# Key scores spread to step 84 of a batch, with the first piece's query scores all behind them

## The chip, the cores and the metric

The kernel runs on one core of one Trainium2 chip. The metric is the device time of one execution in microseconds, the median of several runs.

## The reference

For each of four batches the reference computes an attention through 49 agents, and then a feed-forward layer with a cosine gate over all 49,920 rows. Cut to what matters:

```python
def sm(a, b):
    s = scale * (a @ b.transpose(0, 2, 1))
    s = s - s.max(-1, keepdims=True)
    e = np.exp(s)
    return e / (e.sum(-1, keepdims=True) + 1e-09)
a2k = sm(agents, k)            # 49 x 12480 in each batch
agent_v = a2k @ v
q2a = sm(q, agents)            # 12480 x 49 in each batch
x = (q2a @ agent_v)            # all batches: 49920 x 128
h = x @ w_in                   # 49920 x 2048
return (h * np.cos(h)) @ w_out
```

## The kernel before

The 12,480 rows of a batch are cut into 13 groups of 960. The feed-forward layer runs as one long loop of 832 steps: a group takes 16 steps (two halves of 480 rows, eight pairs of 128-wide slices of the 2048 columns), and a batch takes 208. In this text a step is counted from the start of its batch, and eight steps that begin at a multiple of eight are called an octet, by the number of their first step.

In each step TensorE makes two products `ph` (the 2048-wide layer, with `w_in` already folded into the agents' values), ScalarE takes the cosine `c` of them, VectorE makes `r = (c - 1) * ph`, and four steps later TensorE multiplies `r` by `w_out` into `po`. Once in eight steps two further products (`po<-pT,b`) add what was subtracted. `ph` has three buffers in PSUM, so TensorE can be at most three steps ahead of VectorE.

Between the steps stands the attention, written out by hand into a table of steps:

- Key scores of the next batch: 13 jobs, one for each group. A job has two halves (`part_scores`, L232), each of four matmuls into the one PSUM tile `one` (`ps_1`, a single buffer, L610). After the second half ScalarE copies the scores to `s`, and VectorE updates the running maximum `run`.
- Query scores: the same two halves. ScalarE copies them to `e`, VectorE finds each row's maximum `mx` (`query_ranked`, L686) and GpSimd subtracts it. In the four steps of a burst VectorE does both straight from PSUM (`query_kept`, L673).
- The maxima's chain: `top` reduces `run` to `m` on VectorE, `across` transposes it on TensorE into `one`, VectorE makes `mx` and `mxw` of it, `spread` multiplies it back into `one`, and VectorE copies it to `mxb`. Then GpSimd subtracts `mxb` from all 13 groups of `s` (`shift`, L392).
- At step 112 (24 or 26 in a first part, 8 in later batches) comes a burst: ScalarE leaves the cosine for the exponentials of a whole piece of queries and, at step 112, of all key groups, with a table load before and after.

`plan` puts a call at a fixed step. `job` puts it in a queue with a first step and a due step; `spread_over` hands out such steps evenly. A queue entry may begin only in steps whose place in the octet is 0, 1, 2, 4 or 6 (`free`, L1114), one half at a time, the one with the earliest due step first. Inside each engine the order of instructions is the order in which the table is run. `early[b]` is the piece of queries whose burst is at step 112 of batch b; two of its six groups are made in the burst before, and the other four are the first piece's query scores of which the change speaks. The fourth batch has no next batch, and the changed lines leave it as it was.

Of the kernel before, what the change touches and what calls it, by code (L numbers as in the profile page):

```python
# [37 lines left out]
S0 = 24  # L38
T1 = 112
T2 = 8  # L40
K1 = 76
V1 = 196
NV = 5
WL = 19
# [1 line left out]
SH = 1  # L46
# [26 lines left out]
QP = 1  # L73
QD = 1
EA = 0
QS = 0
QV = 1
PJ = 1
QI = 5
# [43 lines left out]
N0 = 2  # L123
N1 = 4
N2 = 2
# [19 lines left out]
def agent_attention_cos_ffn(ctx, tc, qT, kT, v, agT, w_in, w_out, outT):  # L145
    nc = tc.nc
    NB, _, N = qT.shape
# [8 lines left out]
    NG = N // GRP  # L156
# [31 lines left out]
    pe, dve, act, pool = (Ordered(x) for x in (nc.tensor, nc.vector, nc.scalar, nc.gpsimd))  # L188
# [122 lines left out]
    class Agents:  # L311
# [42 lines left out]
            self.rank(g)  # L354

        def rank(self, g):
            if g == 0:
                dve.tensor_copy(self.run, self.part(g))
            else:
                dve.tensor_max(self.run, self.run, self.part(g))  # L360
# [5 lines left out]
            return self.s[:, g * GT:(g + n) * GT, :]  # L366

        def top(self):
            self.m = self.sb.tile([TT, NA], F32, name="m", bufs=1)
            dve.tensor_reduce(self.m, self.run.rearrange("p t a -> p a t"), axis=AX.X, op=ALU.max)  # L370

# [166 lines left out]
    class First(Fast):  # L538
# [30 lines left out]
                dve.tensor_reduce(self.m[:, 0], self.run.rearrange("p t a -> p a t"), axis=AX.X, op=ALU.max)  # L569

        def top(self):
            dve.tensor_max(self.m[:, 0], self.m[:, 0], self.m[:, 1])

        def across(self, pt):
# [32 lines left out]
    with ExitStack() as pools:  # L607
# [388 lines left out]
        plan, post = Plan(), Plan()  # L996
# [3 lines left out]
        def job(n, *parts, by=10 ** 6):  # L1000

            queue.append((n, len(queue), by, parts))

        def spread_over(lo, hi, by, jobs):

            for i, parts in enumerate(jobs):
                job(lo + (hi - lo) * i / len(jobs), *parts, by=lo + (by - lo) * (i + 1) / len(jobs) + 1)

        def q_lot(n):
            return [(query, n, k, piece_of[n]) for k in range(2)]  # L1010
# [8 lines left out]
        def burst(n, piece, two=(), ab=None, also=()):  # L1019

            shut.update(range(n, n + SHUT))
            wide_at.update(range(n, n + SHUT + WX))
            for i in range(0, len(two), 2):
                post(n + i // 2 * BD, query_two, two[i:i + 2], piece_of[two[0]])
            if ab is not None:
                for g, k in lots:
                    post(n, pinned_exp, ab, g, k)
            post(n, query_exp, piece)
            if also:
                post(n, query_exp, also)  # L1030
                post(n + 12, query_sums, also, 0, len(also))
                post(n + 20, query_inverse, also, 0, len(also))
            s0 = SF if ab is not None else SD1
            for k in piece[:s0]:
                post(n, query_sum, k)
            post(n, query_inverse, piece, 0, s0)
            m = n + SM
            if ab is not None:
                for k in piece[s0:]:
                    post(m, query_sum, k)  # L1040
                    m += 1
                post(m, query_inverse, piece, s0, len(piece))
                return
            for i in range(s0, len(piece), ST):
                j = min(i + ST, len(piece))
                post(m, query_sums, piece, i, j)
                m += 1
            post(m + (SR if n < T3 + (NB - 1) * PER else SZ), query_inverse, piece, s0, len(piece))
# [12 lines left out]

        plan(K1 + 10, fill_ones)
        for n, k in enumerate(LC):
# [4 lines left out]
        early = [pieces[2 * b + 2] for b in range(NB)]  # L1068
# [3 lines left out]
        for b in range(NB):  # L1072
            o = b * PER
            go, stop = o + (T1 if b < NB - 1 else T3), o + PER + T2
            last = OG and b == NB - 2
            if BM and b:
                for c in range(DFF // 512):
                    if b < NB - 1 or not BZ >> c & 1:
                        post(o + BM + 3 * c, big_late)
            if OG and b == NB - 1:  # L1080
                break
            k0 = o + (T2 + K0 if b else KB)
            spread_over(k0 + (QS if b < NB - 1 else 0), go - 5, go - 1, [q_lot(n) for n in early[b][N2 if b else N0:]])
            if b == NB - 1:
                burst(go, early[b])
                for c in range(DFF // 512):
                    if BZ >> c & 1:
                        post(go, big_late)
                for i in range(FB):
                    post(go + FO, keep_warm)  # L1090
                break
            nxt = ab[b + 1]
            spread_over(k0, o + K1, o + K1 + 1, [[(nxt.scores, g, k) for k in range(2)] for g in range(NG)])
            plan(o + K1 + 2, nxt.top)
            job(o + K1 + 4, (nxt.across,), by=o + K1 + 5)
            job(o + K1 + 6, (nxt.spread,), by=o + K1 + 8)
            for g in range(NG):
                plan(o + K1 + 9 + SH * g, nxt.shift, g, 1, pool)
            burst(go, early[b], late[b][:N1], nxt)
            for g in range(0, NG, VP):  # L1100
                at = go + V0 + (o + V1 - go - V0) * g / NG
                job(at, *((nxt.values, x, k) for x in range(g, min(g + VP, NG)) for k in range(2)), by=at + 6 * VP)
            spread_over(go + QV, o + V1 + 8 if last else stop - 3, o + V1 + 8 if last else stop - 1, [q_lot(n) for n in late[b][N1:]])
            if last:
                spread_over(o + V1 + 6, stop - 1, stop - 1, [q_lot(n) for n in early[b + 1][:-2]])
                burst(stop, late[b], early[b + 1][-2:], also=early[b + 1])
            else:
                burst(stop, late[b], early[b + 1][:N2])
            i = (b + 1) % 2
            job(o + V1 + 3, (nxt.inverse,), by=o + V1 + 8)  # L1110
            job(o + V1 + 6, *((nxt.project, c, a[i]) for c in range(DFF // 512)), by=o + PER - 6)
            job(o + V1 + 7, (nxt.project_out, wio, b1[i], b2[i]), by=o + PER + 2)
# [8 lines left out]
        while queue or begun:  # L1121
# [7 lines left out]
            n, i, by, parts = x  # L1129
# [232 lines left out]
```

## Time and profile before

| | |
|---|---|
| median of 3 runs | 1167.57 us (1167.34 to 1168.55) |
| span of the profiled execution | 1171.5 us |
| TensorE matmul busy | 1127.9 us (96%) |
| VectorE busy | 1064.8 us (91%) |
| ScalarE busy | 979.0 us (84%) |
| GpSimd busy | 564.2 us (48%) |
| chain that ended last | TensorE 62%, VectorE 18%, ScalarE 12% |

The span runs from the first to the last instruction of one profiled execution; it is the only time that the page gives of that execution, and it is 3.9 us above the median of the unprofiled runs. Busy shares are averages over the whole program; the loop's stretches differ, so the rows below are taken by octets.

### The profile page before, as it was taken

The numbers are of one execution on the slowest core, as the hardware profiler recorded it, in microseconds if no ns is written. First come the engines' busy times: TensorE is split into PE (matmuls) and PEld (weight loads), VectorE is DVE, ScalarE is ACT, GpSimd is POOL, SyncE is SP. The second block draws the span as 40 slices with busy tenths as digits, with TensorE's granted clock in tenths as the row PEclk, the third lists the DMA queues.
The fourth block names the chain that finished last, engine by engine and source line by source line (L and its number), as shares of the span: only waits on it lengthen the run. The fifth ranks groups of instructions, "written<-read, shape, count | busy, mean of one in ns | idle before, by whom it ended". The sixth has DMA issues, their size and how long they took to land.

```text
span 1171.5 us, 17248 instructions
## 1 busy us (share of the span) xinstructions
PE 1127.9 (96%) x6075; PEld 925.7 (79%) x6075; DVE 1064.8 (91%) x1202; ACT 979.0 (84%) x1267; POOL 564.2 (48%) x725
## 2 busy tenths in 40 slices
PE   8989999999999999999999999999999999999996
PEld 8869888778887888777887788877888767767774
DVE  5689888989998999989999899998999899999997
ACT  3467877889889878898888888798988999999996
POOL 2012321758963311539894331175896455545551
PEclk9899999999999999999999999999999999999999
DMA  8733433143331333124241233214331100000001
GB/s 328 304 123 119 135 102 115 55 138 105 90 113 51 103 108 120 52 87 121 78 133 53 85 102 114 89 51 138 101 94 55 49 18 34 34 18 34 17 34 37
DMA packets 31631, 109.44 MB, mean 93 GB/s; under 512 B 3504, under 2 KB 4016, under 8 KB 31536
## 3 DMA queue, kind: packets, MB, share of 16 engines
q1 hardware_dynamic: 31392, 108.13, 28.5%
q8 instruction: 50, 0.82, 0.3%
q14 instruction: 45, 0.37, 0.1%
q10 hardware_dynamic: 144, 0.12, 0.0%
HBM read 82.68 MB, written 25.56 MB: 92 GB/s over the span
## 4 chain that ended last, share of the span: by engine, by line
PE 62%; DVE 18%; ACT 12%; issue 5%; DMA 1%; POOL 1%; SPq 0%; ACTq 0%; DVEq 0%
PE ph L182 26%; PE po L182 24%; DVE r L182 13%; PE one L182 13%; ACT c L182 7%; DVE rz L182 2%; ACT osb L182 1%; ACT s L182 1%; ACT e L182 1%; ACT p L182 1%; ACT L182 1%; DVE sums L182 1%; DMA c<-kT 1%; DVE e L182 1%; DMA vh<-v 1%
## 5 line engine op out<-in xcount | busy, mean ns | idle before, releaser
L182 DVE SCALAR_TENSOR_TENSOR r<-c,ph 128x960 fp32r<-128x960 f32 (+1 forms) x833 | 906.4, 1134 | 43.3 <-ACT c L182 36.5
L182 ACT ACTIVATE c<-ph 128x960 f32<-128x960 f32 x832 | 784.8, 977 | 136.6 <-PE ph L182 120.7
L182 PE MATMUL ph<-pT,a 113*128 113x480 f32 x1664 | 519.2, 393 | 16.9 <-DVE r L182 13.1
L182 PE MATMUL po<-r,w 128*128 128x480 f32 x1664 | 523.3, 396 | 5.1 <-ACT osb L182 4.9
L182 PEld LDWEIGHTS ph<-pT,a 113*128 113x128 f32 x1664 | 295.2, 189 | 129.5 <-DVE r L182 65.3
L182 PEld LDWEIGHTS po<-r,w 128*128 128x128 f32 x1664 | 292.1, 189 | 51.4 <-ACT osb L182 13.6
L182 POOL CAST pT<-p 49x480 fp32r<-49x480 f32 x102 | 59.4, 582 | 259.7 <-ACT p L182 256.9
L182 PEld LDWEIGHTS one<-ag,xt 128*120 128x120 f32 x1088 | 133.9, 184 | 12.3 <-DVE sums L182 1.5
L182 PE MATMUL one<-ag,xt 128*120 128x98 f32 x1088 | 134.4, 265 | 0.7 <-DVE b L182 0.5
L182 POOL TENSOR_TENSOR pT<-p,pT 49x480 fp32r<-49x480 f32 x102 | 124.2, 1218 | 8.2
L182 POOL TENSOR_TENSOR vh<-vt,vh 120x512 fp32r<-120x512 f32 x78 | 93.4, 1198 | 30.5 <-ACT vh L182 30.5
L182 POOL TENSOR_TENSOR p<-e,rz 120x392 f32<-120x392 f32 x51 | 43.7, 856 | 55.2 <-DVE rz L182 50.8
L182 POOL TENSOR_TENSOR e<-e,mx 120x392 f32<-120x392 f32 x25 | 21.2, 847 | 86.5 <-DVE mx L182 86.5
L182 PE MATMUL po<-pT,b 113*128 113x480 f32 x208 | 62.5, 382 | 0.0
L182 POOL TENSOR_TENSOR raw<-c,raw 128x480 f32<-128x480 f32 x23 | 28.3, 1231 | 69.9 <-ACT raw L182 69.8
L182 ACT COPY osb<-po 128x480 f32<-128x480 f32 x104 | 58.0, 557 | 2.2 <-PE po L182 2.2
L182 PEld LDWEIGHTS ph<-ag,xt 128*120 128x120 f32 x480 | 51.9, 185 | 7.2 <-DVE r L182 4.4
L182 PE MATMUL ph<-ag,xt 128*120 128x98 f32 x480 | 54.2, 269 | 2.7 <-DVE r L182 2.0
L182 PEld LDWEIGHTS one<-vh,eh 120*113 120x113 f32 x312 | 45.9, 177 | 8.3 <-POOL vh L182 2.5
L182 PE MATMUL one<-vh,eh 120*113 120x258 f32 x312 | 50.8, 284 | 1.4 <-DVE e L182 1.4
L182 POOL TENSOR_TENSOR eh<-s,eh 120x196 fp32r<-120x196 f32 x78 | 47.7, 612 | 6.3
L182 POOL CAST eh<-s 120x196 fp32r<-120x196 f32 x78 | 27.8, 356 | 32.7 <-ACT s L182 32.3
(137 smaller groups left out, 746.4 us busy)
## 6 DMA issues: line engine op xcount, KB each, us to landing
xt<-qT SPq DMA_DIRECT2D x52, 480.0 KB, 3.5
outT<-osb SPq DMA_DIRECT2D x51, 480.0 KB, 2.6
xt<-kT SPq DMA_DIRECT2D x46, 480.0 KB, 3.6
vt<-v SPq DMA_DIRECT2D x43, 512.0 KB, 3.9
c<-kT SPq DMA_DIRECT2D x6, 480.0 KB, 7.0
vh<-v SPq DMA_DIRECT2D x5, 512.0 KB, 8.0
raw<-w_in SPq DMA_DIRECT2D x2, 512.0 KB, 7.1
a<-w_in SPq DMA_DIRECT2D x2, 512.0 KB, 6.7
```

What stands on the lines that cost most here:

```text
L182: ins = f(*args, **kw)
```

## The change

The spread of the key scores ends at step 84 instead of 76. The four query groups of the first piece, which were spread over the same steps as the key scores, now begin at step 84. The chain of the maxima starts eight steps later with it and has one step more between `top` and `across` and two more between `across` and `spread`'s first step; the shifts begin at step 95 instead of 85. Nothing is computed in another way. The assertions only check that all groups have been ranked when `top` is built.

```diff
-K1 = 76
+K1 = 84
...
-QS = 0
+Q0 = 84
...
         def rank(self, g):
+            self.ranks = g + 1
...
         def top(self):
+            assert self.ranks == NG
...
             k0 = o + (T2 + K0 if b else KB)
-            spread_over(k0 + (QS if b < NB - 1 else 0), go - 5, go - 1, [q_lot(n) for n in early[b][N2 if b else N0:]])
+            spread_over(o + Q0 if b < NB - 1 else k0, go - 5, go - 1, [q_lot(n) for n in early[b][N2 if b else N0:]])
...
             spread_over(k0, o + K1, o + K1 + 1, [[(nxt.scores, g, k) for k in range(2)] for g in range(NG)])
-            plan(o + K1 + 2, nxt.top)
-            job(o + K1 + 4, (nxt.across,), by=o + K1 + 5)
-            job(o + K1 + 6, (nxt.spread,), by=o + K1 + 8)
+            k1 = o + K1
+            plan(k1 + 2, nxt.top)
+            job(k1 + 5, (nxt.across,), by=k1 + 6)
+            job(k1 + 8, (nxt.spread,), by=k1 + 10)
             for g in range(NG):
-                plan(o + K1 + 9 + SH * g, nxt.shift, g, 1, pool)
+                plan(k1 + 11 + SH * g, nxt.shift, g, 1, pool)
```

TensorE, batch 1 (the second), where the chain stands. Before, from step 79 on; `ph` and `po` are the loop's products, `one<-ident,m` is `across`, `one<-ident,mxw` is `spread`:

```order
L182 MATMUL ph<-pT_96,a_701 128x480 x2
L182 MATMUL po<-r,w_70 128x480 x2
L182 MATMUL ph<-pT_94,a_701 128x480 x2
L182 MATMUL one<-ident,m 49x120
L182 MATMUL po<-r,w_70 128x480 x2
L182 MATMUL ph<-pT_94,a_701 128x480 x2
L182 MATMUL po<-r,w_70 128x480 x2
L182 MATMUL ph<-pT_94,a_701 128x480 x2
L182 MATMUL one<-ident,mxw 120x49
```

and in the changed kernel, from step 88 to 92; `one<-ag,xt` is half a score job:

```order
L182 MATMUL one<-ag,xt 120x98 x4
L182 MATMUL po<-r,w_70 128x480 x2
L182 MATMUL ph<-pT_94,a_701 128x480 x2
L182 MATMUL one<-ident,m 49x120
L182 MATMUL po<-r,w_70 128x480 x2
L182 MATMUL ph<-pT_94,a_701 128x480 x2
L182 MATMUL one<-ag,xt 120x98 x4
L182 MATMUL po<-r,w_70 128x480 x2
L182 MATMUL ph<-pT_94,a_701 128x480 x2
```

Before, nothing but the loop stood around `across` and `spread`; now a half of a query's scores stands before `across` and the next job's half one step behind it, `one` being the same buffer, and `spread` follows three further steps on.

TensorE, batch 1, the last sixteen steps before the burst at step 112. Before, from step 96 to 100, only the loop and one transposition `one<-ident,p` of a query group's weights:

```order
L182 MATMUL ph<-pT_95,a_701 128x480 x2
L182 MATMUL po<-r,w_70 128x480 x2
L182 MATMUL ph<-pT_95,a_701 128x480 x2
L182 MATMUL po<-pT_94,b_91 128x480
L182 MATMUL po<-pT_94,b_93 128x480
L182 MATMUL po<-r,w_70 128x480 x2
L182 MATMUL ph<-pT_95,a_701 128x480 x2
L182 MATMUL one<-ident,p_100 113x120 x4
```

and in the changed kernel:

```order
L182 MATMUL ph<-pT_95,a_701 128x480 x2
L182 MATMUL one<-ag,xt 120x98 x4
L182 MATMUL po<-r,w_70 128x480 x2
L182 MATMUL ph<-pT_95,a_701 128x480 x2
L182 MATMUL one<-ag,xt 120x98 x4
L182 MATMUL po<-r,w_70 128x480 x2
L182 MATMUL ph<-pT_95,a_701 128x480 x2
L182 MATMUL po<-r,w_70 128x480 x2
L182 MATMUL ph<-pT_95,a_701 128x480 x2
L182 MATMUL po<-pT_94,b_91 128x480
L182 MATMUL po<-pT_94,b_93 128x480
```

Octets 96 and 104 held no score half and now hold three and one.

GpSimd, batch 1, the shifts (`s<-s,mxb`) and the query subtractions (`e<-e,mx`) among the writes of a group's weights `pT` and `p`. Before:

```order
L182 TENSOR_TENSOR s<-s,mxb 120x392 x4
L182 TENSOR_TENSOR e<-e,mx_4919 120x392
L182 TENSOR_TENSOR s<-s,mxb 120x392 x4
L182 TENSOR_TENSOR p_100<-e,rz_2324 120x2x4x49
L182 TENSOR_TENSOR s<-s,mxb 120x392 x5
```

and in the changed kernel:

```order
L182 TENSOR_TENSOR s<-s,mxb 120x392 x3
L182 TENSOR_TENSOR e<-e,mx_4990 120x392
L182 TENSOR_TENSOR s<-s,mxb 120x392 x3
L182 CAST pT_96<-p 49x480
L182 TENSOR_TENSOR pT_96<-p,pT_96 49x480
L182 CAST pT_96<-p 49x480
L182 TENSOR_TENSOR pT_96<-p,pT_96 49x480
L182 TENSOR_TENSOR s<-s,mxb 120x392 x4
L182 TENSOR_TENSOR e<-e,mx_5092 120x392
L182 TENSOR_TENSOR s<-s,mxb 120x392 x3
L182 TENSOR_TENSOR p_101<-e,rz_2325 120x2x4x49
```

The shifts now stand around the four writes of the group that begins at step 112, and two query subtractions stand among them instead of one.

## Rows read from the trace of the kernel before

**Rows 1.** The page's first part: busy us, share of span, instructions.

```profile
PE 1127.9 (96%) x6075; PEld 925.7 (79%) x6075; DVE 1064.8 (91%) x1202; ACT 979.0 (84%) x1267; POOL 564.2 (48%) x725
```

**Rows 2.** Windows, batch 1, octets: length, then busy of the engines named.

```profile
core 0: us, PE busy (x) PEld busy (x) DVE busy (x) ACT busy (x) POOL busy (x), PEclk, DMA share, GB/s
390.04:401.37 11.33, 11.33 (x73) 10.21 (x71) 10.16 (x12) 9.09 (x14) 3.09 (x4) 1.00 0.41 132
...
411.99:422.46 10.47, 10.47 (x65) 9.41 (x63) 9.63 (x11) 8.60 (x12) 3.08 (x4) 1.00 0.28 94
422.46:434.13 11.67, 11.67 (x77) 10.56 (x75) 11.50 (x14) 9.05 (x13) 1.35 (x2) 1.00 0.36 97
434.13:445.02 10.89, 10.89 (x68) 9.69 (x67) 10.41 (x14) 8.71 (x12) 0.84 (x1) 1.00 0.43 133
445.02:455.57 10.55, 10.55 (x65) 9.32 (x64) 9.59 (x10) 8.64 (x13) 4.45 (x5) 1.00 0.26 85
...
477.45:487.99 10.54, 10.24 (x52) 8.02 (x52) 10.08 (x12) 8.32 (x11) 3.11 (x4) 1.00 0.12 47
487.99:497.14 9.15, 8.79 (x43) 7.04 (x42) 8.96 (x9) 8.14 (x11) 9.07 (x11) 1.00 0.19 54
497.14:505.90 8.76, 8.70 (x39) 6.57 (x38) 8.59 (x9) 8.31 (x10) 7.58 (x10) 1.00 0.15 58
505.90:514.77 8.87, 8.48 (x34) 5.64 (x32) 8.70 (x9) 7.95 (x9) 1.88 (x2) 1.00 0.00 1
sum 124.73, PE 123.36 PEld 103.64 DVE 116.75 ACT 103.31 POOL 41.10; mean PE 10.28 PEld 8.64 DVE 9.73 ACT 8.61 POOL 3.42
```

**Rows 3.** Timeline, TensorE, steps 24 and 25 of batch 1: start, length.

```profile
400.72 0.60 PE L182 MATMUL ph<-pT,a 113*128 113x480 f32 x2
...
402.45 0.59 PE L182 MATMUL ph<-pT,a 113*128 113x480 f32 x2
...
403.32 0.39 PE L182 MATMUL ph<-pT,a 113*128 113x480 f32 x1
```

**Rows 4.** Groups of instructions, steps 24 to 111 of batch 1: busy, mean ns.

```profile
L182 DVE TENSOR_TENSOR run<-run,s 120x392 f32<-120x392 f32 x11 | 6.2, 567 | 2.9 <-ACT s L182 2.6
L182 DVE TENSOR_REDUCE mx<-e 120x8 f32<-120x392 f32 x3 | 1.7, 554 | 0.0
```

**Rows 5.** Windows, batch 0, octets 24, 80, 88 and the sum of eleven.

```profile
112.86:128.35 15.49, 14.97 (x105) 13.39 (x103) 13.89 (x18) 13.89 (x20) 8.94 (x13) 1.00 0.46 127
...
196.58:207.92 11.34, 10.37 (x60) 8.83 (x58) 10.32 (x13) 8.68 (x12) 4.45 (x6) 1.00 0.25 87
207.92:218.78 10.86, 10.49 (x59) 8.73 (x58) 9.71 (x10) 8.70 (x13) 10.78 (x17) 1.00 0.31 92
...
sum 123.53, PE 121.21 PEld 104.43 DVE 111.42 ACT 101.28 POOL 46.17; mean PE 11.02 PEld 9.49 DVE 10.13 ACT 9.21 POOL 4.20
```

**Rows 6.** Waits, batch 0, 198 to 203 us: total, times, longest.

```profile
PE one L182 <- DVE mxw L182: 1.0, 1, 1.0
```

**Rows 7.** Timeline behind the burst at batch 1's step 8, TensorE.

```profile
384.09 0.71 PE L182 MATMUL ph<-pT,a 113*128 113x480 f32 x2 [1.31 <-DVE r L182]
```

**Rows 8.** Timeline behind the burst in batch 0, VectorE.

```profile
124.21 0.56 DVE L182 TENSOR_REDUCE mx<-one 120x8 f32<-120x392 f32 x1
124.81 0.57 DVE L182 TENSOR_TENSOR e<-one,mx 120x392 f32<-120x392 f32 x1
```

**Rows 9.** Timeline, GpSimd, up to the burst at step 112 of batch 1.

```profile
497.49 4.66 POOL L182 TENSOR_TENSOR s<-s,mxb 120x392 f32<-120x392 f32 x5
503.10 0.58 POOL L182 CAST pT<-p 49x480 fp32r<-49x480 f32 x1 [0.96 <-ACT p L182]
503.76 1.22 POOL L182 TENSOR_TENSOR pT<-p,pT 49x480 fp32r<-49x480 f32 x1
...
518.63 0.35 POOL L182 CAST eh<-s 120x196 fp32r<-120x196 f32 x1 [10.78 <-ACT s L182]
```

**Rows 10.** Timeline, ScalarE: the key groups' exponentials in that burst.

```profile
517.06 4.64 ACT L182 ACTIVATE s<-s 120x1568 f32<-120x1568 f32 x3
```

More of the change, by code (lines that the diff above doesn't have):

```diff
@@ L571, in top @@
         def top(self):
+            assert self.ranks == NG - 1
             dve.tensor_max(self.m[:, 0], self.m[:, 0], self.m[:, 1])
```

## The prediction

> **What bounds the kernel now.** I read the page's first part, then the loop by octets. The page calls TensorE the fullest engine, VectorE next [rows 1]; neither share tells what a score half costs. The octets of batch 1 do. Octet 104 holds nothing but the loop and takes 8.87 us, with VectorE busy for 8.70 of it: it runs at VectorE's pace, 1.09 us a step. Octet 40 holds five score halves and takes 11.67 us, with TensorE busy throughout: it runs at TensorE's pace [rows 2]. The price of a half on TensorE is seen in two neighbouring steps: from one `ph` to the next 1.73 us with a half between, 0.87 us without [rows 3]. So a half costs 0.84 to 0.86; I take 0.84, and a bare octet of TensorE work is then 8 x 0.88 + 0.44 for the two `po<-pT,b` = 7.48. Check: 7.48 + 5 x 0.84 = 11.68 against 11.67. Octet 16 has four halves and a transposition, 11.33 [rows 2], so a transposition is 11.33 - 10.84 = about 0.5.
>
> VectorE's sum is 8.66 to 8.87 plus 0.57 for each `run` and 0.55 for each `mx` [rows 4], that is 0.28 per half. The two engines' sums cross near two halves in an octet: the first half in a bare octet is nearly free, the third costs its full 0.84. Octet 88, with one half and one `mx`, shows it: 9.15, only 0.28 above the bare 8.87 [rows 2].
>
> The Trainium skill, Perfetto Trace Analysis, section Identifying the Most-Contended Engine, says that matmul busy time is a poor measure of headroom and that weight-load busy time should be used. The trace agrees: from octet 40 to octet 104 the weight loads fall from 10.56 to 5.64 us, the matmuls only from 11.67 to 8.48. By matmul busy time octet 104 would have 0.39 us of room and its first half would cost about 0.45; by the row of octet 88 it costs 0.28.
>
> **What the change does to the stretch.** Steps 88 to 111 held one half in batch 1 (three in batch 0) and now hold seven. They come from the earlier octets. No instruction is added or removed, so the total on each engine stays; all that can change is how much of it lies beside the other engine's work. I write n for halves, T for a transposition, and give each octet of the changed order the measured time of an octet of before with the same content and much the same places; where there is none I count steps: 1.72 with a half, 1.39 with T, 0.9 for the first bare step behind one, 1.09 for each further bare step, 0.44 more for `po<-pT,b`.
>
> *Batch 1, octets 16 to 104, before 124.73 [rows 2].* 16: n 4 to 2 with T, counted 10.35. 24: n 3 to 4, as octet 48, 10.89. 32: n 3 to 2 with T, counted 10.15. 40 and 48: n 5 and 4 to 3 and 3, but VectorE keeps its four reductions of `big` there; their VectorE times fall from 11.50 and 10.41 by one `run` and one `mx` to 20.8 together, while the count of steps with the reductions in bare steps gives 22.2: I take 21.6. 56: as before, 10.55. 64: n 5 to 2 with T, counted 10.0. 72: three halves at its head, as octet 88 of batch 0, 10.86 [rows 5]. 80: n 3 and T, as octet 32, 10.47. 88: n 3 with `across` and `spread`, 7.48 + 2.52 + 0.55 = 10.55, and 0.4 for the wait discussed below, 10.95. 96: n 3 and T, 10.47, where 8.76 stood. 104: n 1, 9.15, where 8.87 stood. Sum 125.44: **0.7 slower**.
>
> So filling the sparse end gains there: seven halves in place of one, six more, cost 3.8 instead of 5.0 in octets 88 to 104 (30.57 against 26.78). But octets 16, 32, 40, 48 and 64 are themselves thinned below the crossing point, and give back less than 0.84 a half.
>
> *Octet 8 of batch 1* loses one half at step 11. TensorE made it while VectorE was behind after the burst, and then still waited 1.31 us for `r` [rows 7]. I give nothing back for it.
>
> *Second way.* For each octet take the larger of the two engines' sums. Batch 1: before 122.9, after 123.5, so +0.5; what was measured beyond the sums (1.8) contains the chain's stall: octet 80 takes 10.54 where TensorE's sum is 7.48 + 0.84 + 0.5 + 0.6 = 9.4 [rows 2]. Of that 1.1 I expect 0.3 to remain, since `across` and `spread` now stand five steps apart and VectorE has its results long before. That gives +0.5 - 0.8 = **0.3 faster**. Between the two ways I take the middle, +0.2, for batch 1, and the same for batch 2, whose table is the same. Bounds: 1.3 faster (every octet at its sums, 123.5 against 124.7) to 1.3 slower (first way with 40 and 48 at 22.2).
>
> *Batch 0, octets 24 to 104, before 123.53 [rows 5].* Octet 24 loses two halves just behind its burst, and with them a maximum and a subtraction that VectorE made straight from PSUM, 0.56 + 0.57 [rows 8]. TensorE's share was hidden behind the burst; VectorE's was not, since it trails there (busy 13.89 of 15.49 [rows 5], the rest at the burst's head): 15.49 - 1.13 = 14.36. The others as above: 32 and 48 with n 5, 11.67 each; 40, 56 and 64 with n 3 and T, 10.55 each; 72 n 4, 10.89; 80 10.47, where 11.34 stood with the chain's stall; 88 10.95; 96 10.47; 104 9.15. Sum 121.28: 2.2 faster. Second way: the sums go from 120.5 to 120.1, and 0.8 of the chain's stall goes: 1.2 faster. I take 1.7 faster, bounds 0.9 and 3.4 (all octets at their sums).
>
> *GpSimd.* The shifts start some eight to ten steps later. From `mxb` at step 93 or 94 GpSimd has 13 shifts of 0.93 (4.66 for five), two query subtractions of about 0.9, four `pT` writes (twice 0.58 + 1.22) [rows 9], and a wait of some 3 us for the `mx` of the query scored at step 97, behind which the other shifts are queued: about 20.6 us in all. From there to step 112 it is 2 + 10.5 + 9.2 = 22 us, and the key groups' exponentials start two to three microseconds after that step. Before, GpSimd stood idle 10.78 us at that place [rows 9]. The third lot of exponentials, which needs the last shifts, starts 3 us into the 4.64 [rows 10]. Cover: some 6 us. I cost it at nothing; if it were gone, ScalarE's exponentials and every cosine behind them would wait, microsecond for microsecond, in three batches.
>
> *Loads.* The four query loads move behind the key loads on SP's queue, one in four to seven steps; no TensorE wait for a load stands among the long ones now, and the last is due at step 102, not at 88. Nothing.
>
> Sum: -1.7 + 2 x 0.2 = -1.3 us. In the profiled execution's terms 1171.5 would become 1170.2; the runs' median lies 3.9 below that span, so 1167.57 - 1.3 = **1166.3**.
>
> **Rivals.**
>
> *Faster: the octets run at their sums.* If the small misalignments of before do not return in the new order, the gain is 3.4 + 1.3 + 1.3 = 6.0 us, 1161.6. For: the five- and four-half octets do run at their sums [rows 2], and the halves lie more evenly. Against: batch 1's octets as a whole were 1.8 above them.
>
> *Slower: the chain stalls inside a full stretch.* `one` is a single buffer. The half behind `across` cannot start until VectorE has read `across`'s result, and on VectorE that read now stands behind `r` of step 88 and the rank `mx` of a query (0.55). By the rows I get 0.4 us. In batch 0 such a wait was 1.0 at `spread` [rows 6], in a sparse place. If it is 2 us or more per batch now, with TensorE the bound around it, the gain of the chain (0.8) is lost and 1 us or more comes on top: -1.3 + 3 x 1.8 = +4.1, 1171.7; it decides from about 1.6 us per chain on. Against it: VectorE's sum over steps 88 to 90 is 4.3, below TensorE's 4.5.
>
> *Slower by GpSimd,* as priced above; it needs some 6 us of lateness that I do not find.
>
> **Chances.** A measurement of this kernel can tell about 0.2% (2.3 us) from no change. Forecast, within 0.2%: 0.50. Octets at their sums, or far enough towards them to pass 2.3 us: 0.34. The chain's stall: 0.13, GpSimd 0.03. Range 1162.0 to 1169.8: down to nearly the whole of the faster rival, up to the likeliest with the slow bounds of all batches (-0.9 + 2.6 = +1.7) and a little of the stall. The likeliest case's own range is 1165.3 to 1169.3.
>
> **What would show it.** Right: octet 96 near 10.5 and 104 near 9.2 in all three batches; octet 64 of batch 1 near 10.0 and not 9.1; octets 40 and 48 of batch 1 together above 21; octet 24 of batch 0 near 14.4; no wait of a microsecond between `across` and the half behind it; GpSimd idle by several microseconds before its first `eh` in the burst, and the burst at step 112 as long as before, about 19.5 us. Wrong: thinned octets that give back 0.84 for each half (then it is the faster rival), ScalarE waiting for GpSimd in the burst, or TensorE waiting for `mx` at step 90.

## The result and the profile after

The changed kernel takes 1175.27 us (median of 5, 1173.06 to 1180.64) where the kernel before takes 1168.15 (median of 5, 1167.34 to 1168.91): ratio 1.0069, 95% interval 1.0055 to 1.0084. It is slower by 0.7%, outside the predicted range, and its runs lie 7.6 us apart where those of before lie 1.6 apart. About 5 us of that spread belong to the slowest run, 1180.64 us, which is the profiled one: its clock also fell ahead of the loop (last section).

The profiled execution has a span of 1178.9 us against 1171.5. The windows of the octets of batch 1 in the changed kernel, cut as in [rows 2]; columns are the length, then the busy time and count of each engine, then the granted clock:

```profile
393.09:403.15 10.06, 9.96 (x57) 8.41 (x55) 9.63 (x12) 8.69 (x12) 2.61 (x4) 1.00 0.39 135
...
414.02:424.23 10.21, 10.14 (x57) 8.26 (x55) 9.32 (x10) 8.79 (x13) 0.74 (x2) 1.00 0.39 135
424.23:435.92 11.69, 10.89 (x61) 8.62 (x59) 11.57 (x13) 8.53 (x12) 3.69 (x4) 1.00 0.14 42
435.92:447.01 11.09, 10.26 (x60) 8.86 (x59) 10.41 (x14) 8.60 (x11) 0.00 (x0) 1.00 0.33 99
...
457.56:467.54 9.98, 9.88 (x57) 8.47 (x55) 9.34 (x9) 8.57 (x13) 3.09 (x4) 1.00 0.30 100
...
478.47:488.90 10.43, 10.43 (x65) 9.39 (x63) 9.58 (x11) 8.59 (x11) 3.05 (x4) 1.00 0.28 96
488.90:500.50 11.60, 10.89 (x64) 9.11 (x62) 11.26 (x14) 8.70 (x12) 3.54 (x5) 1.00 0.29 85
500.50:510.98 10.48, 10.48 (x65) 9.42 (x63) 9.56 (x10) 8.61 (x13) 8.12 (x10) 1.00 0.29 96
510.98:520.14 9.16, 8.78 (x42) 6.67 (x40) 8.96 (x9) 8.14 (x11) 9.00 (x11) 1.00 0.18 54
sum 127.05, PE 123.62 PEld 105.06 DVE 118.56 ACT 103.17 POOL 41.44; mean PE 10.30 PEld 8.75 DVE 9.88 ACT 8.60 POOL 3.45
```

The reader should compare octet 40 (424.23) with its row in [rows 2]: two halves fewer, TensorE busy for 0.78 us less, and the octet is as long as before, with VectorE busy for 11.57 of 11.69. The twelve octets take 127.05 us against 124.73; 2.3 us are lost here, and as much in batch 2. In batch 0 the eleven octets from 24 take 125.03 against 123.53 [rows 5], and the whole loss is in octet 24, the one with the burst:

```profile
112.90:129.88 16.98, 14.79 (x89) 13.04 (x87) 13.32 (x16) 13.97 (x20) 8.92 (x13) 0.90 0.30 88
...
184.91:196.26 11.35, 11.09 (x69) 9.70 (x67) 10.21 (x11) 8.69 (x11) 3.66 (x4) 1.00 0.22 53
...
206.73:218.29 11.56, 10.88 (x64) 9.11 (x62) 11.22 (x14) 8.70 (x12) 3.50 (x9) 1.00 0.28 85
...
sum 125.03, PE 121.49 PEld 106.26 DVE 112.04 ACT 101.19 POOL 46.58; mean PE 11.04 PEld 9.66 DVE 10.19 ACT 9.20 POOL 4.23
```

The number behind the five engines, the granted clock of TensorE, is 0.90 in octet 24: it fell there. Windows around the burst at step 8 of batch 1 show the same:

```profile
382.40:387.10 4.70, 2.55 (x16) 2.01 (x15) 4.63 (x7) 3.90 (x5) 4.20 (x8) 1.00 0.11 43
387.20:390.50 3.30, 3.30 (x11) 2.74 (x10) 2.33 (x3) 1.28 (x3) 0.00 (x0) 0.50 0.00 0
390.60:394.00 3.40, 3.40 (x21) 2.87 (x20) 2.42 (x4) 2.94 (x4) 0.00 (x0) 1.00 0.46 136
```

TensorE first waits; then, for 3.3 us, it runs at 0.50 of its clock, 1.2 GHz, makes half as many matmuls, and is back at 2.4 GHz. Its wait is in the timeline of the same place, where [rows 7] had 1.31:

```profile
385.60 0.70 PE L182 MATMUL ph<-pT,a 113*128 113x480 f32 x2 [2.15 <-DVE r L182]
```

In batch 2 the same wait of 2.14 us passes without a fall, and octet 8 takes 15.80 us there against 17.35 in batch 1. So the fall comes in some executions of the place and not in others.

Batch 0 shows the wait as well: TensorE idles 2.19 us in octet 24, where before it has no idle time there over 0.8 us. Timelines of the changed kernel, octet 24 of batch 0 and octet 8 of batch 2:

```profile
123.66 0.71 PE L182 MATMUL po<-r,w 128*128 128x480 f32 x2 [2.19 <-ACT osb L182]
667.94 0.70 PE L182 MATMUL ph<-pT,a 113*128 113x480 f32 x2 [2.14 <-DVE r L182]
```

One more thing differs. Timelines of the changed kernel, GpSimd and VectorE in octet 40 of batch 1:

```profile
427.29 0.85 POOL L182 TENSOR_TENSOR p<-e,rz 120x392 f32<-120x392 f32 x1
...
427.32 1.23 DVE L182 TENSOR_TENSOR run<-run,s 120x392 f32<-120x392 f32 x1
```

and behind `across` in octet 88, where `mx<-e` is the rank of a query and `mx<-one` the read of `across`:

```profile
491.50 0.57 DVE L182 TENSOR_REDUCE mx<-e 120x8 f32<-120x392 f32 x1
...
491.96 0.26 DVE L182 TENSOR_REDUCE mx<-one 49x1 f32<-49x120 f32 x1
492.21 0.84 POOL L182 TENSOR_TENSOR e<-e,mx 120x392 f32<-120x392 f32 x1 [2.78 <-DVE mx L182]
492.26 0.87 DVE L182 COPY mxw<-mx 49x120 f32<-49x120 f32 x1
492.28 0.91 PEld L182 LDWEIGHTS one<-ag,xt 128*120 128x120 f32 x8 [1.11 <-DVE mx L182]
492.28 1.08 PE L182 MATMUL one<-ag,xt 128*120 128x98 f32 x8 [0.71 <-DVE mx L182]
```

`run` takes 1.23 us instead of 0.57 [rows 4], and `mxw` 0.87 instead of the 0.21 that it takes in the kernel before, where no GpSimd instruction stands beside it:

```profile
479.70 0.21 DVE L182 COPY mxw<-mx 49x120 f32<-49x120 f32 x1
```

Each begins 0.02 to 0.07 us behind a GpSimd product or subtraction and ends only after it. There are six such places in the changed kernel (`run` at step 73 of batch 0 and at step 41 of batches 1 and 2, `mxw` at step 90 of all three), and in the kernel before neither `run` nor `mxw` is lengthened anywhere. Meetings as such are not new: seven other VectorE instructions (six on `rz`, one on `s`) are lengthened in both kernels alike.

VectorE's total shows the six. The first part of the page of the changed kernel, against 1064.8 us in [rows 1], and of the kernel with both edits of the ports run below:

```profile
PE 1128.3 (96%) x6075; PEld 930.1 (79%) x6075; DVE 1068.6 (91%) x1201; ACT 978.4 (83%) x1268; POOL 563.8 (48%) x726
PE 1124.5 (96%) x6107; PEld 928.8 (80%) x6107; DVE 1064.6 (91%) x1201; ACT 978.0 (84%) x1268; POOL 564.0 (48%) x726
```

What a longer instruction costs is another question. In octet 88 TensorE is busy for 10.89 of 11.60 us, and its one idle time is the 0.71 in front of the score half. The half waits for `mx<-one`, which ends before `mxw` begins and is itself not lengthened; it is late because the rank `mx<-e` stands in front of it. So the wait comes from that order on VectorE, and no wait of TensorE in this octet goes back to the longer `mxw`.

### The profile page after: what moved, and what is told of

It is laid out like the page before. It is cut to its first block, busy times and chain, and to the rows that moved or that the text cites. A ratio compares the mean times of both kernels' runs of the same rounds, so it can differ in the third digit from the quotient of the medians.

```text
span 1178.9 us, 17245 instructions
## 1 busy us (share of the span) xinstructions
PE 1128.3 (96%) x6075; PEld 930.1 (79%) x6075; DVE 1068.6 (91%) x1201; ACT 978.4 (83%) x1268; POOL 563.8 (48%) x726
## 4 chain that ended last, share of the span: by engine, by line
PE 57%; DVE 22%; ACT 13%; issue 5%; DMA 1%; POOL 1%; SPq 0%; ACTq 0%; DVEq 0%
PE ph L182 24%; PE po L182 21%; DVE r L182 16%; PE one L182 12%; ACT c L182 7%; DVE rz L182 2%; ACT osb L182 1%; ACT s L182 1%; ACT p L182 1%; ACT e L182 1%; DVE sums L182 1%; ACT L182 1%; DMA c<-kT 1%; DVE e L182 1%; DMA vh<-v 1%
## 5 line engine op out<-in xcount | busy, mean ns | idle before, releaser
L182 DVE TENSOR_TENSOR run<-run,s 120x392 f32<-120x392 f32 x47 | 28.6, 608 | 17.4 <-ACT s L182 15.9
```

The costliest lines, as they stand in the source:

```text
L182: ins = f(*args, **kw)
```

## The experiments

All ratios are against the kernel before on the same chip, with their 95% interval. The first four runs were made on one chip and the other four on a second; the kernel before has the median 1167.67 us on both.

Three theories stood behind the runs. G: the halves taken away behind the bursts leave TensorE waiting, and its clock falls. P: VectorE and GpSimd instructions now meet, and this costs time. B: the reductions of `big` make VectorE the bound in octets that lost halves. The rival of each is that the octets are slow because they are thin, with nothing more to it.

**Halves put back behind the bursts.** Two unused halves in batch 0, one each in batches 1 and 2.

```diff
+        plan(S0 + 3, keep_warm)
+        plan(S0 + 4, keep_warm)
+        for b in range(1, NB - 1):
+            plan(b * PER + T2 + 3, keep_warm)
```

> The changed kernel, with unused score halves (four matmuls, results never read) put back where the change took halves away: two at steps 27 and 28 of batch 0, one at step 11 of batches 1 and 2, just behind the bursts. Theory G (the change leaves TensorE waiting over 2 us behind a burst, and the granted clock then falls to 0.5 for 3.4 us in some executions): no clock fall inside the loop, octet 24 of batch 0 at most 15.5 us, octet 8 of batch 1 at 15.8 instead of 17.35, the runs of the kernel within 1.5 us of each other, median 1170 to 1172.5. Theory O (the loss is in the octets 16 to 111, the clock fall is chance and has nothing to do with the halves): the median stays within 1 us of 1175 and the runs spread over several us as before.

Measured 1172.47 us (1171.33 to 1172.83), ratio 1.0041 (1.0029 to 1.0054). With more work the kernel is 2.8 us faster than the changed one by the medians, and its runs lie 1.5 us apart. The windows of the two burst octets and of the twelve that follow:

```profile
107.57:122.95 15.38, 14.86 (x105) 13.54 (x103) 13.24 (x16) 13.84 (x20) 8.87 (x13) 1.00 0.35 97
368.85:384.66 15.81, 14.16 (x91) 12.44 (x92) 13.62 (x17) 13.81 (x20) 6.40 (x9) 1.00 0.27 71
...
384.66:511.71 127.05, 123.63 (x691) 105.03 (x689) 118.53 (x125) 103.17 (x131) 41.46 (x47) 1.00 0.28 89
```

The clock stays at 1.00, and the other octets of the three batches are within 0.06 us of the changed kernel's. G holds; what it does not explain is the 127.05. The other profiles say the same. There are three such burst octets in each: octet 24 of batch 0 and octet 8 of batches 1 and 2. In the two kernels without the halves (the changed one and queries alone, below) the clock fell in four of six; in the kernel before and the seven runs with halves there, in none of 24.

**The first query group left behind the burst.**

```diff
-            spread_over(o + Q0 if b < NB - 1 else k0, go - 5, go - 1, [...])
+            lots_q = [q_lot(n) for n in early[b][N2 if b else N0:]]
+            if b < NB - 1:
+                spread_over(k0, k0 + 1, k0 + 1, lots_q[:1])
+                spread_over(o + Q0, go - 5, go - 1, lots_q[1:])
...
```

> The changed kernel, but the first of the four query groups stays where it was before the change, just behind the burst (steps 27 and 28, or 11 and 12); the other three begin at step 84. Theory G: no clock fall inside the loop, octet 24 of batch 0 near 15.5, octet 8 near 15.8, and the octets 16 to 111 as in the changed kernel but for one half more in 16 and two fewer in 88 to 104; median 1170 to 1172. Theory O: 1174 to 1176.

Measured 1170.02 us (1169.04 to 1171.54), ratio 1.0019 (1.0009 to 1.0029). Real halves do what the unused ones did, and one group fewer at the end of the stretch gains further: octets 88 and 96 of batch 1 take 11.01 and 9.61 us where the run before had 11.56 and 10.47, and octet 16 takes 0.76 more.

**Keys alone, queries alone.** In the first the query line is as before, in the second only the query line is changed.

```diff
-            spread_over(o + Q0 if b < NB - 1 else k0, go - 5, go - 1, [...])
+            spread_over(k0, go - 5, go - 1, [...])
```

> Only the key scores are spread to step 84, with the later chain and shifts; the query scores are spread over the batch as before. The halves behind the bursts are back. Theory G: no clock fall, narrow spread; octets 96 and 104 bare again (8.8 each); octets 40 and 48 of batch 1 still slow, 23 us together, because the reductions of `big` stand there in bare steps; about 1.9 us slower than before in batches 1 and 2, median 1170 to 1172.5. Theory Q (it is the late queries that cost, in the octets 88 to 104 with the chain among them): within 1 us of before, 1168.

```diff
-            spread_over(k0 + (QS if b < NB - 1 else 0), go - 5, go - 1, [...])
+            spread_over(o + 84 if b < NB - 1 else k0, go - 5, go - 1, [...])
```

> Only the query scores are put behind step 84; key scores to step 76, chain and shifts as before. The halves behind the bursts are gone, but no query stands around across. Theory G: the clock falls in some executions, runs spread by 3 us and more, burst octets of 17 us where it does; octets 16 to 104 of batch 1 about 126.4 against 124.7; median 1172 to 1176. Theory K (it is the later keys and chain that cost): within 1 us of before, 1168, and a narrow spread.

Keys alone: 1170.57 us (1168.54 to 1171.98), ratio 1.0027 (1.0016 to 1.0038). Queries alone: 1173.32 us (1171.79 to 1177.09), ratio 1.0059 (1.0042 to 1.0075). Each half of the change loses by itself, so neither Q nor K holds. Of the two profiles, only the one without halves behind the bursts has falls of the clock inside the loop. Its windows of the burst octets of batches 0 and 1 hold both cases in one execution, and the third line, octets 16 to 104 of batch 1, is near the 126.4 that I expected:

```profile
107.09:122.50 15.41, 13.21 (x89) 11.71 (x87) 13.24 (x16) 13.86 (x21) 8.91 (x13) 1.00 0.34 97
368.51:385.89 17.38, 14.88 (x85) 12.87 (x85) 13.68 (x17) 14.02 (x20) 6.42 (x9) 0.90 0.24 65
385.89:512.32 126.43, 124.06 (x691) 104.64 (x689) 117.63 (x125) 103.07 (x131) 41.73 (x47) 1.00 0.28 89
```

Octet 24 without its two halves, without VectorE's share of them, and without a fall takes 15.41 us: 0.08 less than before. VectorE's timeline there tells why:

```profile
120.02 2.22 DVE L182 SCALAR_TENSOR_TENSOR r<-c,ph 128x960 fp32r<-128x960 f32 x2 [0.17 <-ACT c L182]
122.63 1.16 DVE L182 SCALAR_TENSOR_TENSOR r<-c,ph 128x960 fp32r<-128x960 f32 x1 [0.39 <-ACT c L182]
```

Rid of the maximum and the subtraction, VectorE waits for ScalarE's cosines instead. Behind the burst the first four of these start 9.28, 10.59, 11.93 and 12.81 us into the octet, and in the kernel before 9.28, 10.58, 11.93 and 12.81.

**The meetings of VectorE and GpSimd undone.** On the run with the halves put back: `run` one `r` later where it met a product, and one ranking two steps later, so that GpSimd's subtraction starts after `mxw`.

```diff
-            self.rank(g)
+            if step[0] in (74, PER + 41, PER + 42, 2 * PER + 41, 2 * PER + 42, 73):
+                post(step[0], self.rank, g)
+            else:
+                self.rank(g)
...
-                post(step[0] + QD - 1, query_ranked, n)
+                post(step[0] + QD - 1 + 2 * (step[0] % PER == 88), query_ranked, n)
```

> The first repair (unused halves behind the bursts) with two things moved that put a VectorE instruction beside a GpSimd one: the update of run at step 41 of batches 1 and 2 and at step 73 of batch 0 comes one r later, and the ranking of the query scored at step 88 comes two steps later, behind mxw. No work is added or removed. Theory P (run and mxw take 0.65 us longer because GpSimd is in a subtraction or product at that moment): run 0.57 and mxw 0.21 us at these places, octet 88 near 10.9 instead of 11.56 in three batches, octet 72 of batch 0 near 10.9 instead of 11.38, octet 40 of batches 1 and 2 near 11.2 instead of 11.70; about 3.3 us less in all, median near 1169. Theory V (VectorE simply has too much to do in these octets): less than 1 us less, median 1171.5 to 1172.5.

The second edit alone:

> Of the former only the ranking behind mxw. Theory P: octet 88 near 10.9 in the three batches, octets 40 and 72 as in the first repair (11.70, 11.38); about 1.9 us less, median near 1170.5. Theory V: no octet changes by more than 0.2.

Both: 1168.48 us (1167.51 to 1169.23), ratio 1.0004 (0.9995 to 1.0013). The second alone: 1171.14 us (1170.01 to 1172.09), ratio 1.0029 (1.0018 to 1.0041). The same work in the same octets takes 4.0 us less than with the halves put back alone, 2.7 of it by the first edit and 1.3 by the second, where I had expected 1.9 of the second. Timeline and windows of octets 40 and 88 of batch 1 with both edits:

```profile
418.15 0.84 POOL L182 TENSOR_TENSOR p<-e,rz 120x392 f32<-120x392 f32 x1
419.04 0.68 DVE L182 TENSOR_REDUCE big<-a 113x1 f32<-113x512 f32 x1
419.64 0.56 DVE L182 TENSOR_TENSOR run<-run,s 120x392 f32<-120x392 f32 x1
...
481.49 0.26 DVE L182 TENSOR_REDUCE mx<-one 49x1 f32<-49x120 f32 x1
481.78 0.21 DVE L182 COPY mxw<-mx 49x120 f32<-49x120 f32 x1
481.80 1.08 PE L182 MATMUL one<-ag,xt 128*120 128x98 f32 x8 [0.19 <-DVE mx L182]
```
```profile
415.07:425.90 10.83, 10.63 (x61) 8.63 (x59) 10.83 (x13) 8.43 (x12) 3.70 (x4) 1.00 0.15 45
478.92:490.03 11.11, 10.92 (x64) 9.13 (x62) 10.57 (x14) 8.70 (x12) 3.51 (x5) 1.00 0.28 88
```

`run` is back at 0.56 and `mxw` at 0.21, octet 40 falls from 11.70 to 10.83 and octet 88 from 11.56 to 11.11. V is out: no work was taken away, yet VectorE's total is back at 1064.6 us, and the runs are 4.0 us shorter.

The two edits show different things. The first undoes the three meetings at `run`, in octets where TensorE waited for `r` behind them (0.29 and 0.51 us in octet 40 of the changed kernel, none with the edit), and P holds there. It also moves `run` one place back, and what that alone is worth was not tried. The second edit moves the rank out from in front of `across`'s read as well as away from `mxw`. TensorE's busy time in octet 88 stays at 10.9 and its wait falls from 0.71 to 0.19, about as much as the octet; so by the trace the gain is the earlier read, and P is not shown for `mxw`. (In the split run TensorE waits 1.00 us for an `r` in this octet instead; whether the longer `mxw` costs there was not separated.)

**The reductions of `big` moved** from steps 38 to 47 to steps 57, 60, 97 and 101, again with the halves put back.

```diff
-                        post(o + BM + 3 * c, big_late)
+                        post(o + ([57, 60, 97, 101][c] if b < NB - 1 else BM + 3 * c), big_late)
```

> The first repair, with the four reductions of big of batches 1 and 2 moved from steps 38 to 47 to steps 57, 60, 97 and 101, where more score halves stand beside them. Theory B (in the thinned octets 32 to 48 these reductions make VectorE the bound): octets 32, 40 and 48 of batch 1 together fall from 32.99 to about 30.5, octets 56 and 96 rise by 0.3 or less each; about 2 us less per batch, median near 1168.5. Theory T (the thinning itself costs, each bare step at VectorE's pace): the three octets fall by less than 1 us.

Measured 1171.14 us (1170.03 to 1175.87), ratio 1.0031 (1.0022 to 1.0040): 1.3 us less, where I expected 4. The windows of octets 40, 48, 56 and 104 of batch 1:

```profile
415.53:426.47 10.94, 10.64 (x61) 8.70 (x59) 10.03 (x10) 8.43 (x12) 3.70 (x4) 1.00 0.15 46
426.47:436.79 10.32, 10.26 (x60) 8.86 (x59) 9.49 (x10) 8.61 (x13) 0.00 (x0) 1.00 0.35 108
436.79:447.64 10.85, 10.75 (x65) 9.19 (x63) 10.46 (x12) 8.76 (x12) 4.45 (x5) 1.00 0.24 80
501.09:510.64 9.55, 9.50 (x42) 6.32 (x40) 9.55 (x10) 8.58 (x12) 9.34 (x11) 1.00 0.18 51
```

Octets 40 and 48 lose some 0.76 us each, octet 32 nothing, and 56 and 104 take 0.3 and 0.4 of it back. B holds for the three octets (1.5 less), and at less than half of the size that I gave it for the batch.

**All together:** the first query group behind the burst, both moves of the ports run, and the moved reductions.

> The first query group behind the burst (as in the split run), both moves of the ports run, and the moved reductions, in one kernel. If P and B hold beside G: 1170.0 - 3.2 - 2 to 4 = 1163 to 1165, faster than the kernel before by 0.2 to 0.4%. If only G holds: 1169 to 1170.

Measured 1164.42 us (1163.20 to 1164.54), ratio 0.9968 (0.9956 to 0.9980): faster than both kernels, and inside the range that I expected. Windows of the eleven octets from 24 in its batch 0 and of the twelve from 16 in its batch 1, where before has 123.53 [rows 5] and 124.73 [rows 2]:

```profile
107.16:227.94 120.78, 119.84 (x713) 104.97 (x711) 110.68 (x120) 100.66 (x131) 45.58 (x59) 1.00 0.33 103
381.62:506.21 124.59, 123.49 (x683) 103.85 (x681) 116.56 (x124) 103.60 (x131) 40.92 (x46) 1.00 0.27 88
```

Nearly all of the gain over the kernel before is in batch 0 (2.75 us); batch 1 gains 0.14. In batches 1 and 2 the repairs thus pay for the change and little more. What the moved reductions would do to the kernel before was not tried.

## Why the prediction was wrong, point by point

The stretch from the start of the loop's first cosine to that of its last, in the profiles, splits the loss; beside it stand the medians of the runs:

| kernel | loop, us | less than the row above | median, us | less |
|---|---|---|---|---|
| changed | 1090.89 | | 1175.27 | |
| halves put back: no fall of the clock | 1087.86 | 3.0 | 1172.47 | 2.8 |
| and the rank behind `mxw` | 1086.39 | 1.5 | 1171.14 | 1.3 |
| and `run` moved | 1084.29 | 2.1 | 1168.48 | 2.7 |
| before | 1083.37 | 0.9 | 1167.67 | 0.8 |

**A step that failed outright** is "No instruction is added or removed, so the total on each engine stays", and with it "GpSimd. ... I cost it at nothing". VectorE's total rose by 3.8 us, from 1064.8 to 1068.6. The step on GpSimd asked only whether the shifts end in time. They did: the last ends just before the burst, and GpSimd then idles 3.56 us in batch 1, as GpSimd's timeline up to the burst shows, the counterpart of [rows 9]:

```profile
516.84 2.80 POOL L182 TENSOR_TENSOR s<-s,mxb 120x392 f32<-120x392 f32 x3
519.59 0.85 POOL L182 TENSOR_TENSOR p<-e,rz 120x392 f32<-120x392 f32 x1
524.00 0.35 POOL L182 CAST eh<-s 120x196 fp32r<-120x196 f32 x1 [3.56 <-ACT s L182]
```

What I did not ask is what stands beside GpSimd's instructions on VectorE at their new times. Six meetings lengthen VectorE's instructions by about 0.65 us each. The three at `run` cost 2.1 us of the loop, by the run that moves `run`; the three at `mxw` cost nothing that the trace shows. The Trainium skill, SBUF — State Buffer, section Who interferes with whom, has the rule: VectorE and GpSimd share one pair of ports, a VectorE instruction with two inputs in SBUF meets a GpSimd instruction that reads SBUF, some copies meet any, and whoever comes second waits for the whole of the other. The trace agrees in the main: `run` has two inputs in SBUF, begins behind the product and ends at 428.55 us, 0.41 after the product's end at 428.14. A wait for the whole of the product would make that 0.57, the length of `run` alone. That rule spoke against this change, and I did not weigh it.

**"I give nothing back for it"** (octet 8) was right for the halves' own time, 15.80 us where the clock held. But the row on which it rested, a wait of 1.31 us, grows to 2.15 when the half in front of it is gone, and I named no price for a longer wait of TensorE. In octet 24 of batch 0 the same happens. This is the largest single cause: two falls and 3.0 us in the profiled execution, 2.8 us in the median by the first repair. The Trainium skill, TensorE: Matmul & The Clock Gate, section What's actually happening, says that the clock is gated by how busy TensorE has been and has only the two levels; the windows agree with 1.00 and 0.50. Which executions fall stays open, and so does why batch 2 of the changed kernel was spared with the same wait.

**Octet 24 of batch 0, "15.49 - 1.13 = 14.36"** failed as well. Without the halves and the two VectorE instructions it takes 15.41 us where the clock holds. The step took VectorE to be the engine that trails behind the burst. But ScalarE's cosines come at the same times with and without that work, and VectorE only waits for them longer. This term alone is 1.05 us.

**Octets 40 and 48, "I take 21.6"**: 22.78 measured, and 21.93 without the meeting at `run`, between the 21.6 and the upper count of 22.2. The meeting and the reductions of `big` are not separate prices: octet 40 takes 11.70 with both, 10.94 without its reductions, 10.83 without the meeting and 10.47 with neither. Octet 72 of batch 0, put at 10.89, took 11.35 with its meeting and 10.85 without.

**Octet 88, 10.95**: 11.60 measured in batch 1. I put the wait in front of the half behind `across` at 0.4 us; it is 0.71 (the place that [rows 6] showed for batch 0), and 11.09 to 11.11 remain when the rank is out of the way. The slower rival named this place, this wait and this rank, and TensorE waiting for `mx` at step 90 was one of its signs. About 0.5 us in each of three batches hang on it. That is less than the 1.6 per chain from which it would have decided, so the rival is one part of the loss.

**What held** is the rest of the table. Octets 16, 32, 64, 80, 96 and 104 of batch 1 were put at 10.35, 10.15, 10.0, 10.47, 10.47 and 9.15; they took 10.06, 10.21, 9.98, 10.43, 10.48 and 9.16. So did its conclusion: the sparse end takes the halves cheaply, and the thinned octets give back less than was taken from them. With the clock held, `run` moved and the rank out of the way, the change stands at 1.0004 (0.9995 to 1.0013), inside the "within 0.2%" of the forecast. The sum itself was not right even there: -1.3 us was forecast, and the loop is 0.9 longer. Batch 0 gains 1.06 instead of 1.7, and batches 1 and 2 lose 0.99 and 0.92 instead of 0.2 each. For these two the first way, counting octets, said 0.7 slower and was near; the middle with the second way was not. The faster rival, all octets at their sums, a gain of 6.0 us, did not come about in any run.

By the profiles the loss in the loop, 7.5 us, is the clock (3.0), the meetings at `run` (2.1), the late read of `across` (1.5) and a balance of octets 0.9 to the bad. The reductions of `big`, moved alone, give back 1.3 in the median, in part from the same octets as the meetings.

## What to carry to other kernels

When a schedule moves work on GpSimd, or moves VectorE's small instructions past it, write down for each VectorE instruction with two SBUF inputs, and for each SBUF copy, what GpSimd does at that moment: an instruction of 0.2 to 0.6 us became one of 0.9 to 1.2 here. Then ask what waits behind it: in the changed kernel `run` held up TensorE, the longer `mxw` did not. Work that fills a wait of TensorE may be free twice over: taking it away returns none of its time, and may cost the clock. The granted clock of each stretch shows it. The spread between runs is a weaker sign, since a fall ahead of the loop spreads them as well.

## What the runs showed that was not expected

A wait of 2.15 us on TensorE behind a burst was followed by 3.3 us at half clock and cost about 1.55 us (17.35 against 15.80), while waits of 1.30 to 1.32 us at the same place, in eight profiles, were not followed by a fall in any. Adding 4 to 8 unused matmuls per burst made the kernel 2.8 us faster.

The profiled execution of before, from which all of the prediction's rows come, has another such fall ahead of the loop, and so has that of the changed kernel. The same window of before, of the changed kernel, and of the run with all together, the granted clock again behind the five engines:

```profile
30.00:60.00 30.00, 27.89 (x195) 26.32 (x194) 20.95 (x47) 12.98 (x41) 1.20 (x1) 0.83 0.77 296
30.00:60.00 30.00, 27.74 (x193) 26.16 (x193) 20.93 (x47) 12.83 (x41) 1.20 (x1) 0.83 0.76 296
30.00:60.00 30.00, 27.59 (x234) 25.86 (x234) 25.88 (x57) 16.51 (x47) 1.20 (x1) 1.00 0.77 295
```

With 0.83 instead of 1.00 TensorE makes 195 matmuls in this window instead of 234, and every later step of those two executions lies some 5 to 6 us later (the loop begins at 76.7 us in both kernels' profiles, at 70.6 to 71.6 in the experiments'). That is why the span of 1171.5 us stood above the median of the runs. A run's time on record is 1.7 to 1.9 us longer than its own span, so the profiled execution of before would count as some 1173.3 us, about 5.7 above the median. A fall at the start of an execution shifts its span, and not the lengths of the octets from which the sum was made. It can spread the runs, whatever the schedule: among the runs of before beside the first four experiments, one takes 1172.88 us at a mean clock of 0.993 where the median is 1167.67, and one with the moved reductions takes 1175.87 at 0.993. Both fit such a fall, as the profile of before has the same 0.993; their own traces are not at hand.
